# A linear-attention and MLP block: duplicated 64-row tails in one DMA, and a new order of the first loads and key projections

## The chip, the cores and the metric

The kernel runs on one core of a Trainium2 chip. The metric is the device time of one execution in microseconds. Each kernel is timed in several runs, and the median is given. A separate, profiled execution supplies the trace.

## The reference

Two blocks work on the same x (2048 tokens, 576 features) and are mixed by a gate. All numbers are float32.

```python
def _A_ref(x, wqkv, wo):                       # 32 heads of 18
    qkv = (x @ wqkv).reshape(B, S, 3, H, Dh).transpose(2, 0, 3, 1, 4)
    q, k, v = qkv[0], qkv[1], qkv[2]
    phi = lambda t: jnp.where(t > 0, t + 1, jnp.exp(t)) + 1e-6
    pq, pk = phi(q), phi(k)
    kv = jnp.einsum("bhsd,bhse->bhde", pk, v)
    z = jnp.einsum("bhsd->bhd", pk)
    o = jnp.einsum("bhqd,bhde->bhqe", pq, kv) / (jnp.einsum("bhqd,bhd->bhq", pq, z)[..., None] + 1e-6)
    return o.transpose(0, 2, 1, 3).reshape(B, S, D) @ wo
def _B_ref(x, w1, b1, w2, b2):                 # 576 -> 4608 -> 576
    h = _gelu(_layernorm(x) @ w1 + b1)
    return h @ w2 + b2
g = _sigmoid((x * gate_w).sum(-1, keepdims=True))
return g * _A_ref(...) + (1 - g) * _B_ref(...)
```

## The kernel before, in words

**Stages.** The kernel first projects x to keys and queries, 16 tiles of 128 tokens one after the other, and sums keys against x on the way; from those sums it makes the attention matrix. The MLP follows, in a scheme with seven products in place of eight; it takes most of the time, and its order of instructions comes from a planner in the program. The change lies in the first 30 us or so and in the loads of the x tiles.

**Precision.** Each operand of a product is split into a high part, rounded by ScalarE (ACT), and a low part, the remainder, made by VectorE (DVE); three products (high by high, low by high, high by low) are summed in PSUM. `split_x` and `split_w` do that for a tile of x and for a half of a weight.

**Rows.** The 576 features are five blocks along the partitions: four of 128 rows, and a tail of 64. The tail is held twice, in partitions 0 to 63 and 64 to 127, so that one matmul serves two of the three products. `load_twice` (line 146) loads it: two DMAs from the same 64 rows of HBM, one into each half of the partitions. It is used by `load_x` (the tail `xe` of a tile), by `load_w` (the tail `we` of a half of the key or query weights, 288 columns) and by `load_wv`. The main part of a tile comes from `xm`, that of a weight half from `wm`. In the profile the tile of x is called `t`, the raw weights are `s`, and their split forms both lie in `y`. A related helper, `four_times` (line 150), describes 32 rows that are read four times, by an access pattern whose first dimension is 4 with stride 0; it serves `load_pair`, whose tails (`accs<-in_xe`) are loaded in a later stage, and the tails of the MLP weights.

**Order.** Every engine runs its instructions in program order: the class `InOrder` (line 110) records each one, so that nearly all have line 120 in the profile, and tiles tell them apart. DMAs are issued from SyncE's queue (SP), from ACT's, and a few from GpSimd's (POOL). Issues by SP and ACT together take eight completion semaphores in turn, so that the ninth waits for the landing of the first.

**The start.** Line 457 and those after it issue the first loads: the first x tile on SP, the first half of the key weights in pieces on ACT, the table load of ACT, then on SP two more x tiles, the second key half, the two query halves, and two tiles of x by rows (`xn`). A set of products of one tile by one half of a weight is 14 matmuls (`project`; `first_keys` names the tile, the half and the PSUM bank). `first_keys` of three tiles by the first half come first, then the column of the gate is put beside the second key half, that half is split, and its keys follow. For the second key half the operand is 290 columns wide, for the others 288, which tells them apart in the profile. `both_phi` takes the keys of a tile through phi, by ACT and DVE.

Of the kernel before, what the change touches and what calls it, by code (L numbers as in the profile page):

```python
# [93 lines left out]
def raw(ap):  # L94
    return ap.bitcast(F32)
# [31 lines left out]
def tile_gated_mix(ctx: ExitStack, tc: tile.TileContext, x, xm, xe, wm, we, wvm, wve, wo, um, ue, w2, b1, b2, gw, out):  # L127
    nc = tc.nc
    pe, act, dve, pool = (InOrder(tc, e) for e in (nc.tensor, nc.scalar, nc.vector, nc.gpsimd))
# [14 lines left out]
        return ps[:, next(ff_banks)]  # L144

    def load_twice(dst, src, by=sp):
        for half in range(2):
            by.dma_start(dst[half * 64:(half + 1) * 64], src)

    def four_times(ap, half):  # L150

# [45 lines left out]
    QUERY, KEY = range(2)  # L197
    TERMS = ((0, 0), (0, 1), (1, 0))
    W, at_ = {}, 0
    for part in (KEY, QUERY):  # L200
        for half in range(2):
            n = HALF + 2 * (part == KEY and half)
# [20 lines left out]
    def load_w(part, half, pieces=((0, 5),), by=sp):  # L223
        if (part, half) not in wraw:
            wraw[part, half] = wsp.tile([P, 5, HALF + 2], F32, name="s", tag="s")
        s = wraw[part, half]
        main = wm[part * 2 + half].rearrange("p (t n) -> p t n", t=4)
        tail = we[part * 2 + half]
        for t0, t1 in pieces:
            if t0 < 4:  # L230
                by.dma_start(s[:, t0:min(t1, 4), :HALF], main[:, t0:min(t1, 4)])
            if t1 == 5:
                load_twice(s[:, 4, :HALF], tail, by)

    def split_w(part, half, by=dve, pieces=((0, 5),)):
        w = W[part, half]
        s = wraw[part, half][:, :, :w.shape[2]]
        for t0, t1 in pieces:
            act.activation(w[:, t0:t1], s[:, t0:t1], AF.Copy)
            by.tensor_tensor(out=w[:, 5 + t0:5 + t1], in0=s[:, t0:t1], in1=raw(w[:, t0:t1]), op=OP.subtract)  # L240

    def load_x(i):
        xraw[i] = yt.tile([P, 5, P], F32, name="t")
        sp.dma_start(xraw[i][:, 0:4], xm[i].rearrange("p (t n) -> p t n", t=4))
        load_twice(xraw[i][:, 4], xe[i])

    def split_x(i, pieces=((0, 5),), on_dve=False):
        if i not in xs:
            xs[i] = x_places[PLACE[i] % X_RING]
        to, src = xs[i], xraw[i]  # L250
        for t0, t1 in pieces:
            if on_dve:
                dve.tensor_copy(to[:, t0:t1], src[:, t0:t1])
            else:
                act.activation(to[:, t0:t1], src[:, t0:t1], AF.Copy)
            if t0 < 4:
                dve.tensor_sub(to[:, 5:9], src[:, 0:4], raw(to[:, 0:4]))
            if t1 == 5:
                dve.scalar_tensor_tensor(to[:, 4], raw(to[:, 4]), low_half[:, 0:1], src[:, 4], op0=OP.mult, op1=OP.add)
# [12 lines left out]
    def project(i, part, half, order=BY_ROWS, n=None, between={}):  # L272
        w = W[part, half]
        p = banks[i, part, half] = ps[:, next(halves_in) if n is None else n]
        for m, (a, b) in enumerate(order):
            pe.matmul(p[:, :w.shape[2]], xs[i][:, a, :], w[:, b], start=(m == 0), stop=(m == len(order) - 1))
            if m in between:
                between[m]()
# [16 lines left out]
    def keys_phi(i, half):  # L295
        if half == 0:
            K[i] = kp.tile([P, D], F32, name="k")
        phi(K[i], i, KEY, half, (lambda: None, lambda: sums_of_x(i))[half])
# [156 lines left out]
    first = ORDER[:FIRST]  # L455
    gwr = spare[0:1, :5 * P]
    load_x(first[0])
    load_w(KEY, 0, ((0, 1), (1, 2), (2, 4)), act)
    pool.dma_start(gwr[:, :D], gw.rearrange("(a n) -> a n", a=1))
    pool.dma_start(gwr[:, D:], gw[4 * P:D].rearrange("(a n) -> a n", a=1))  # L460
    act.activation(tiny, ones[:, 0:1], AF.Exp)
    load_w(KEY, 0, ((4, 5),), act)
    load_x(first[1])
    load_x(first[2])
    load_w(KEY, 1)
    load_w(QUERY, 0)
    load_xn(first[0])
    load_w(QUERY, 1)
# [12 lines left out]
    def first_keys(n, half, between={}):  # L481
        project(first[n], KEY, half, HI_FIRST, 3 * half + n, between)
# [4 lines left out]
    def both_phi(n):  # L487
        for half in range(2):
            keys_phi(first[n], half)
# [13 lines left out]
    first_keys(0, 0, {0: lambda: warm(1), 1: lambda: warm(1), 2: lambda: warm(1), 3: turn_gate})  # L503
    split_x(first[1])
    first_keys(1, 0)
    split_x(first[2])
    first_keys(2, 0)
    dve.tensor_copy(wraw[KEY, 1][:, :, HALF:HALF + 1], column[:, :, None])
    dve.memset(wraw[KEY, 1][:, :, HALF + 1:HALF + 2], 1.0)
    split_w(KEY, 1)  # L510
    load_x(ORDER[3])
    first_keys(0, 1)
    first_keys(1, 1)
    split_w(QUERY, 0)
    both_phi(0)
    first_keys(2, 1)
    both_phi(1)
    keys_split(first[0])
# [54 lines left out]
    def load_wv():  # L573
        sp.dma_start(wv[:, 0:4], wvm.rearrange("p (t n) -> p t n", t=4))
        load_twice(wv[:, 4], wve)
# [1082 lines left out]
```

## Time and profile before

| | |
|---|---|
| median of 3 runs | 1093.72 us (1092.69 to 1094.6) |
| profiled execution | 1095.47 us |
| its span, first to last instruction | 1093.8 us |
| granted TensorE clock, mean | 0.998 |
| PE busy | 1084.9 us (99%) |
| DVE, ACT, POOL busy | 933.3, 692.3, 219.4 us |
| DMA | 189.72 MB, mean 173 GB/s |

PE is TensorE's matmuls, PEld its weight loads, SPq and ACTq are queues that issue DMAs. A row of the timeline gives the start and the length in us, then the engine, line, operation, out<-in by the program's names and how many were merged; in square brackets stands the engine's idle time just before, and what ended it. A row of a table of windows gives, after the window and its length, the busy time of PE, PEld, DVE, ACT and POOL with their instructions in brackets, the granted TensorE clock, the mean busy share of 16 DMA engines, and GB/s.

### The profile page before, as it was taken

The numbers are of one execution on the slowest core, as the hardware profiler recorded it, in microseconds if no ns is written. First come the engines' busy times: TensorE is split into PE (matmuls) and PEld (weight loads), VectorE is DVE, ScalarE is ACT, GpSimd is POOL, SyncE is SP. The second block draws the span as 40 slices with busy tenths as digits, with TensorE's granted clock in tenths as the row PEclk, the third lists the DMA queues.
The fourth block names the chain that finished last, engine by engine and source line by source line (L and its number), as shares of the span: only waits on it lengthen the run. The fifth ranks groups of instructions, "written<-read, shape, count | busy, mean of one in ns | idle before, by whom it ended". The sixth has DMA issues, their size and how long they took to land.

```text
span 1093.8 us, 18578 instructions
## 1 busy us (share of the span) xinstructions
PE 1084.9 (99%) x6712; PEld 998.0 (91%) x6712; DVE 933.3 (85%) x1583; ACT 692.3 (63%) x1228; POOL 219.4 (20%) x212
## 2 busy tenths in 40 slices
PE   8999999999999999999999999999999999999998
PEld 7999999999898989998999989999899998999898
DVE  5568787797699999899999898988887887989888
ACT  5677767444568787787887785555645555455542
POOL 1111112431222321233120221021221221111110
PEclk9999999999999999999999999999999999999999
DMA  6457673654755565744565559664544445444432
GB/s 178 123 98 192 169 176 141 237 217 166 230 181 188 193 218 192 254 174 158 214 216 207 188 192 396 199 233 118 151 132 118 130 123 146 132 121 119 142 90 88
DMA packets 109006, 189.72 MB, mean 173 GB/s; under 512 B 8940, under 2 KB 68604, under 8 KB 104818
## 3 DMA queue, kind: packets, MB, share of 16 engines
q1 hardware_dynamic: 108002, 187.78, 53.6%
q8 instruction: 53, 0.87, 0.4%
q10 hardware_dynamic: 720, 0.74, 0.2%
q14 instruction: 39, 0.32, 0.1%
q0 software_dynamic: 192, 0.01, 0.0%
HBM read 121.70 MB, written 66.80 MB: 172 GB/s over the span
## 4 chain that ended last, share of the span: by engine, by line
PE 96%; ACT 1%; DMA 1%; DVE 1%; issue 0%; SPq 0%; ACTq 0%; DVEq 0%
PE ps L120 96%; DMA s<-in_we 1%; DMA s<-in_wm 0%; ACT e L120 0%; ACT L120 0%; ACT y L120 0%; SPq L120 0%; DVE ks L120 0%; DVE y L120 0%; ACT ks L120 0%; ACTq L120 0%; ACT ys L120 0%; DVE xs L120 0%; DVE wp L120 0%; ACT xn L120 0%
## 5 line engine op out<-in xcount | busy, mean ns | idle before, releaser
L120 PEld LDWEIGHTS ps<-region,h 128*128 128x128 f32 x3072 | 436.5, 188 | 24.5 <-ACT ps L120 0.4
L120 PE MATMUL ps<-region,h 128*128 128x288 f32 x3072 | 452.3, 295 | 0.0
L120 DVE TENSOR_TENSOR accs<-ps,accs 128x576 f32<-128x576 f32 x334 | 245.3, 752 | 25.1 <-PE ps L120 19.4
L120 PE MATMUL ps<-y,wa 128*128 128x512 f32 x1008 | 255.4, 392 | 0.0
L120 PEld LDWEIGHTS ps<-y,wa 128*128 128x128 f32 x1008 | 181.8, 188 | 31.8
L120 PE MATMUL ps<-y,wb 128*128 128x512 f32 x756 | 199.4, 393 | 0.0
L120 DVE TENSOR_TENSOR h<-u,h 128x512 fp32r<-128x512 f32 x240 | 166.0, 711 | 31.5 <-ACT u L120 28.7
L120 POOL TENSOR_TENSOR fresh<-fresh 128x288 f32<-128x288 f32 (+1 forms) x98 | 85.7, 876 | 394.3 <-DVE h L120 167.7
L120 PEld LDWEIGHTS ps<-y,wb 128*128 128x128 f32 x756 | 133.8, 188 | 20.7
L120 PE MATMUL ps<-y 128*128 128x288 f32 (+2 forms) x950 | 135.6, 299 | 4.1 <-ACT y L120 3.3
L120 PEld LDWEIGHTS ps<-y 128*128 128x128 f32 (+1 forms) x950 | 131.2, 190 | 7.0 <-ACT y L120 3.9
L120 ACT ACTIVATE region<-fresh 128x576 fp32r<-128x576 f32 (+1 forms) x132 | 80.3, 625 | 69.3 <-PE ps L120 65.2
L120 POOL TENSOR_TENSOR u<-u 128x512 f32<-128x512 f32 x54 | 72.2, 1337 | 221.7 <-DVE h L120 140.0
L120 ACT ACTIVATE ps<-ps 128x576 f32<-128x576 f32 (+1 forms) x125 | 77.5, 623 | 50.8 <-PE ps L120 36.2
L120 DVE TENSOR_TENSOR region<-fresh,region 128x576 fp32r<-128x576 f32 (+1 forms) x132 | 88.9, 692 | 2.1 <-ACT region L120 2.0
L120 ACT ACTIVATE u<-ps 128x512 f32<-128x512 f32 x73 | 43.4, 594 | 69.4 <-PE ps L120 67.4
L120 ACT ACTIVATE h<-u 128x512 fp32r<-128x512 f32 x128 | 75.0, 620 | 9.4 <-POOL u L120 4.8
L120 ACT ACTIVATE h<-u,b1s 128x512 fp32r<-128x512 f32 x73 | 52.6, 722 | 35.6 <-DVE u L120 35.5
L120 PE MATMUL ps<-wp,qt 128*128 128x288 f32 x448 | 63.0, 297 | 0.0
L120 PEld LDWEIGHTS ps<-wp,qt 128*128 128x128 f32 x448 | 59.8, 188 | 0.0
L120 DVE TENSOR_TENSOR u<-ps,u 128x512 f32<-128x512 f32 x74 | 50.5, 683 | 6.3 <-ACT u L120 5.1
L120 DVE TENSOR_TENSOR u<-u 128x512 f32<-128x512 f32 x74 | 51.4, 695 | 2.5 <-POOL u L120 1.6
(140 smaller groups left out, 1054.3 us busy)
## 6 DMA issues: line engine op xcount, KB each, us to landing
w1d<-wa SPq DMA_DIRECT2D x17, 1280.0 KB
wa<-w1d SPq DMA_DIRECT2D x68, 320.0 KB
fresh<-in_w SPq DMA_DIRECT2D x70, 288.0 KB
y<-yd SPq DMA_DIRECT2D x14, 1280.0 KB
w1d<-wb SPq DMA_DIRECT2D x17, 960.0 KB
wb<-w1d SPq DMA_DIRECT2D x51, 320.0 KB
yd<-ystage SPq DMA_DIRECT2D x28, 320.0 KB
fresh<-in_um SPq DMA_DIRECT2D x64, 128.0 KB
```

What stands on the lines that cost most here:

```text
L120: self.last = self.tc.keep_in_program_order(op(*args, **kwargs))
```

## The change

`load_twice` issues one DMA in place of two: its source pattern gets a first dimension of 2 with stride 0 ahead of the 64 rows. This holds for all 16 x tiles, for the four halves of key and query weights and for the value weights. Pieces 2 to 4 of the first key half go to SP's queue, and the tail of that half moves ahead of ACT's table load. The second key half is issued ahead of the third x tile. The third tile's split and its keys by the first half move behind the second key half's split, and `both_phi` of the first tile ahead of the split of the first query half.

```diff
     def load_twice(dst, src, by=sp):
-        for half in range(2):
-            by.dma_start(dst[half * 64:(half + 1) * 64], src)
+        (ld, r), (st, n) = src.ap
+        by.dma_start(dst, bass.AP(tensor=src.tensor, offset=src.offset, ap=[[0, 2], [ld, r], [st, n]]))
...
     load_x(first[0])
-    load_w(KEY, 0, ((0, 1), (1, 2), (2, 4)), act)
+    load_w(KEY, 0, ((0, 1), (1, 2)), act)
+    load_w(KEY, 0, ((2, 4),))
+    load_w(KEY, 0, ((4, 5),), act)
     pool.dma_start(gwr[:, :D], gw.rearrange("(a n) -> a n", a=1))
     pool.dma_start(gwr[:, D:], gw[4 * P:D].rearrange("(a n) -> a n", a=1))
     act.activation(tiny, ones[:, 0:1], AF.Exp)
-    load_w(KEY, 0, ((4, 5),), act)
     load_x(first[1])
+    load_w(KEY, 1)
     load_x(first[2])
-    load_w(KEY, 1)
     load_w(QUERY, 0)
...
     split_x(first[1])
     first_keys(1, 0)
-    split_x(first[2])
-    first_keys(2, 0)
     dve.tensor_copy(wraw[KEY, 1][:, :, HALF:HALF + 1], column[:, :, None])
     dve.memset(wraw[KEY, 1][:, :, HALF + 1:HALF + 2], 1.0)
     split_w(KEY, 1)
+    split_x(first[2])
     load_x(ORDER[3])
     first_keys(0, 1)
     first_keys(1, 1)
+    both_phi(0)
     split_w(QUERY, 0)
-    both_phi(0)
+    first_keys(2, 0)
     first_keys(2, 1)
```

On SP's queue the start of the program stood like this before; t_168, t_181 and t_185 are the first three x tiles, s_189 is the second key half, s_193 and s_199 are the query halves:

```order
L120 DMA t_168<-in_xm 128x512
L120 DMA t_168<-in_xe 64x128 x2
L120 DMA t_181<-in_xm 128x512
L120 DMA t_181<-in_xe 64x128 x2
L120 DMA t_185<-in_xm 128x512
L120 DMA t_185<-in_xe 64x128 x2
L120 DMA s_189<-in_wm 128x4x288
L120 DMA s_189<-in_we 64x288 x2
L120 DMA s_193<-in_wm 128x4x288
L120 DMA s_193<-in_we 64x288 x2
```

It now stands like this; t_168, t_179 and t_185 are the x tiles, s_171 is the first key half, s_182 the second, s_188 the first query half:

```order
L120 DMA t_168<-in_xm 128x512
L120 DMA t_168<-in_xe 128x1x128
L120 DMA s_171<-in_wm 128x2x288
L120 DMA t_179<-in_xm 128x512
L120 DMA t_179<-in_xe 128x1x128
L120 DMA s_182<-in_wm 128x4x288
L120 DMA s_182<-in_we 128x1x288
L120 DMA t_185<-in_xm 128x512
L120 DMA t_185<-in_xe 128x1x128
L120 DMA s_188<-in_wm 128x4x288
L120 DMA s_188<-in_we 128x1x288
```

Each pair of 64-row transfers has become one of 128 rows, a part of the first key half has come in as the third issue, and the second key half has moved from the tenth and later issues to the sixth and seventh, ahead of the third x.

On PE the projections at the start of the program (288 columns: first key half, or query; 290 columns: second key half) were and are, with the rows of before marked - and those of the change +:

```order
-L120 MATMUL ps<-y 128x288 x38
-L120 MATMUL ps<-y 128x290 x42
+L120 MATMUL ps<-y 128x288 x24
+L120 MATMUL ps<-y 128x290 x28
+L120 MATMUL ps<-y 128x288 x14
+L120 MATMUL ps<-y 128x290 x14
 L120 MATMUL ps<-y 128x288 x42
```

The 14 matmuls of the third tile by the first key half have moved behind 28 of the second key half.

## Prediction

> **What bounds the kernel now.** I read the busy shares first, then the chain that ended last in order of time, then the timelines of TensorE (PE) and of SyncE's queue (SPq) over the first 30 us, then the DMA issues of the first 20 us with their sizes, and last a table of windows with the DMA share. The busy line of the page:
>
> ```profile
> PE 1084.9 (99%) x6712; PEld 998.0 (91%) x6712; DVE 933.3 (85%) x1583; ACT 692.3 (63%) x1228; POOL 219.4 (20%) x212
> ```
>
> PE is the bound. It leaves about 9 us of the span of 1093.8 us idle, so little can be won, and only where PE waits; whatever makes PE later there is paid in full. The chain in order of time (start, length, what) shows where that is:
>
> ```profile
> 9.16 5.51 DMA s<-in_we
> ...
> 14.74 1.42 ACT y L120
> ...
> 16.19 1.68 DVE y L120
> ...
> 17.91 4.35 PE ps L120 x19
> ...
> 28.11 62.01 PE ps L120 x409
> ```
>
> A DMA, the last 64-row tail of the second key half (s<-in_we), is issued at 9.16 and lands at 14.67; ACT and DVE split that weight half in two, PE goes on, and from 28.11 the chain is PE alone. Everything that the change moves lies ahead of that. PE's own timeline:
>
> ```profile
> 8.52 5.32 PE L120 MATMUL ps<-y 128*128 128x288 f32 x38
> 16.21 1.49 PE L120 MATMUL ps<-y 128*128 128x290 f32 x9 [2.37 <-ACT y L120]
> 17.91 9.95 PE L120 MATMUL ps<-y 128*128 128x290 f32 x61 [0.22 <-DVE y L120]
> 28.11 2.13 PE L120 MATMUL ps<-y 128*128 128x288 f32 x14 [0.25 <-DVE accs L120]
> ```
>
> The 38 matmuls end the keys of three tiles with the first key half (14 each), at 5.32/38 = 0.14 us apiece. Then PE stands 2.37 us for the second half, and the 70 matmuls behind it (three tiles by that half, two by the first query half) end at 27.86. So the landing at 14.67 sets the end. Why it is late, SP's queue shows (64-row transfers go out in twos, "x2"):
>
> ```profile
> 4.84 0.74 SPq L120 DMA_DIRECT2D t<-in_xm  x1
> 6.70 1.11 SPq L120 DMA_DIRECT2D t<-in_xe  x2
> 7.85 0.60 SPq L120 DMA_DIRECT2D s<-in_wm  x1
> 8.49 1.27 SPq L120 DMA_DIRECT2D s<-in_we  x2
> ```
>
> The third x stands ahead of the second key half, each issue takes about 0.6 us, and from 5.58 to 6.70 the queue waits. The DMA engines run dry for it (window, length, engines, clock, DMA share, GB/s):
>
> ```profile
> 3.00:4.00 1.00, 1.00 (x6) 1.00 (x6) 0.00 (x0) 0.71 (x2) 0.86 (x4) 1.00 1.00 349
> 6.00:7.00 1.00, 0.84 (x6) 0.65 (x6) 0.99 (x3) 0.75 (x3) 0.00 (x0) 1.00 0.93 176
> 8.00:9.50 1.50, 1.50 (x14) 1.36 (x13) 1.05 (x3) 1.18 (x3) 0.00 (x0) 1.00 0.36 62
> 17.92:21.34 3.42, 3.42 (x14) 3.42 (x15) 2.44 (x3) 3.01 (x9) 0.25 (x1) 0.50 0.62 179
> ```
>
> Full load is 349 GB/s; at 8.0 to 9.5 only 62 GB/s move. The last row is kept for later: after its pause PE runs 3.42 us at clock 0.50.
>
> **The change part by part.** *One transfer for both halves.* It halves the issues of the tails, some 0.55 to 0.6 us of SP time for each, and that looks like the gain. But its source now begins with a dimension of 2 with stride 0. The trace has a relative of it: the loads of accs<-in_xe in a later stage read 32 rows four times with a leading 4. They are issued at 68.31 and 70.26, and this is the DMA load when they are what is left to move:
>
> ```profile
> 68.31 1.28 SPq L120 DMA_DIRECT2D accs<-in_xe  x2
> 70.26 2.32 SPq L120 DMA_DIRECT2D accs<-in_xe  x2
> 73.20:74.20 1.00, 1.00 (x10) 1.00 (x9) 1.00 (x3) 0.77 (x2) 0.00 (x0) 1.00 0.30 79
> ```
>
> A share of 0.30 of 16 engines is four to five of them, and 79 GB/s is less than half of the 176 GB/s and 0.93 at 6 to 7 us, when plain 64-row tails of the same row length are among what moves. I read from this that a leading dimension of 4 puts the transfer on four engines, and that a leading 2, which no row of before has, will put it on two. The Trainium skill goes that step too, in "DMA: Bandwidth & Descriptors", section "Why a DMA increments its semaphore by 16 and not by 1": the hardware's descriptor generator takes the largest number of engines up to 16 that divides the slowest dimension of both access patterns. By that rule the new form gets two engines; the trace's four-fold form agrees with 0.30, and a leading 2 it does not show.
>
> The sizes, by the DMA issues of the first 20 us (KB for each issue, and for one of them the us to its landing):
>
> ```profile
> s<-in_wm SPq DMA_DIRECT2D x3, 576.0 KB
> t<-in_xm SPq DMA_DIRECT2D x4, 256.0 KB
> s<-in_we SPq DMA_DIRECT2D x6, 72.0 KB
> s<-in_wm ACTq DMA_DIRECT2D x2, 144.0 KB
> s<-in_wm ACTq DMA_DIRECT2D x1, 288.0 KB
> t<-in_xe SPq DMA_DIRECT2D x8, 32.0 KB
> accs<-in_gw POOLq DMA_DIRECT2D x1, 2.2 KB, 4.0
> ```
>
> Until the second key half has landed, the changed queue moves main parts of two x and two weight halves, 2*256 + 2*576 = 1664 KB over 16 engines, 104 KB each, and the tails 2*64 + 2*144 = 416 KB over two engines, 208 KB each. The two loaded engines so carry 312 KB, 319.5 thousand bytes; before, with the third x, it is 150 KB on each of 16. One engine moves 349/16 = 21.8 GB/s at full load, 79/4 = 19.8 GB/s by the four-engine row: 14.7 to 16.2 us. SP's issues, seven of 0.6 us, are out by about 5.5 us, so these two engines never run dry. The first packets move at about 2.0 us by this row:
>
> ```profile
> 0.00:2.00 2.00, 0.87 (x4) 0.87 (x5) 0.34 (x5) 0.00 (x0) 1.09 (x11) 1.00 0.05 14
> ```
>
> The second key half then lands at 16.7 to 18.2 us instead of 14.67; I take 17.2, nearer the full-load rate, since wide rows make most of it: **+2.5 us** (+2.0 to +3.5). ACT's 1.42 and DVE's 1.68 behind it stay.
>
> *First weights on two queues.* Pieces 2 to 4 go from ACT's to SP's queue, the tail ahead of ACT's table load. That spares ACT its last issues ahead of the first split, but the first x's tail and this tail now lie on the two engines: 16 + 32 + 36 + 72 = 156 KB, 7.3 us, landed at about 9.3, and the second x 48 KB later, at 11.6. PE's run of 38, which starts at 8.52 now, starts some 2 us later, and the keys of two tiles end by about 15 (16.5 at half clock), ahead of PE's restart at 17.2 + 1.5 = 18.7 (14.67 to 16.21 is 1.5 now). This costs **0**, covered by that wait; without it, it would be the 2 us.
>
> *Second key half ahead of the third x, and the third tile's keys behind it.* Before, 14 matmuls of the third tile by the first half lie ahead of PE's 2.37 us gap; now they lie behind the restart, where PE has no gap: 14*0.14 = **+2.0 us**. In the queue the third x comes 16 + 32 = 48 KB, 2.3 us, after the second key half; its split stands on ACT right behind that half's split and on DVE likewise, and the key phi of the first tile queues behind it. PE reaches the third tile only after 28 matmuls, some 5.8 us after its restart (at the half clock that the window showed): covered.
>
> *What is late next.* The first query half follows with 16 + 32 + 36 + 72 = 156 KB, 7.3 us, after the second key half; its splits, the first two rows below, end 1.41 + 1.66 us later, 10.4 us after that landing. PE is there after 1.5 + 7.7 + 2.0 = 11.2 us (7.7 is 27.86 - 28*0.14 - 16.21): covered by 0.8 us, at the low rate by nothing, but the first nine matmuls of a tile need only the high part, 1.66 us earlier. On ACT the phi of the second and third tile stand behind that split; their banks are not written again before the third tile's queries. Then come an xn of 18 KB and the second query half, 126 KB or 5.9 us more, landed at 30.4; its split (third row) moves from 30.84 to 35.
>
> ```profile
> 17.14 1.41 ACT L120 ACTIVATE y<-s 128x1440 fp32r<-128x1440 f32 x1 [0.98 <-DMA s<-in_we]
> 18.58 1.66 DVE L120 TENSOR_TENSOR y<-s,y 128x1440 fp32r<-128x1440 f32 x1 [0.72 <-ACT y L120]
> 30.84 1.39 ACT L120 ACTIVATE y<-s 128x1440 fp32r<-128x1440 f32 x1
> 16.99 1.11 SPq L120 DMA_DIRECT2D t<-in_xe  x2
> 38.54 0.72 ACT L120 ACTIVATE y<-t 128x640 fp32r<-128x640 f32 x1
> ```
>
> The fourth x (last two rows) is split 20 us after its issue. The two engines' backlog behind the second key half, 140 KB of mains and 208 KB of tails up to that x, is 16.3 us: landed at 33.5, covered. The two short PE waits, 0.22 us here and 0.25 us at 28.11, for ACT and DVE work that has now more time, may go: **-0.2** (0 to -0.5). The half clock came after a pause of 2.37 us; the pause is now 4 us or so, and I leave the 1.7 us that it cost unchanged (bounds: another 1.7, or 1.7 saved).
>
> Sum: 2.5 + 0 + 2.0 - 0.2 = **+4.3 us**. The profiled execution took 1095.47 us with a span of 1093.8, 1.67 us around it; it would take 1099.8. The median of the runs is 1.75 us below it, 1093.72, so I forecast 1098.0. Bounds of the terms: 2.0 + 2.0 - 0.5 - 1.7 = +1.8, and 3.5 + 2.0 + 1.7 = +7.2.
>
> **The rivals.** *All 16 engines still move a tail (faster).* Then the second key half is issued by about 5.4 us and 2080 KB at 349 GB/s take 6.1 us from 2.0 on; allowing from issue to landing the 4.0 us of the small transfer in the sizes above, it lands at about 9.5. PE's gap goes, the half clock with it: 11.2 restart, 84 matmuls of 0.14, end at 23.0 instead of 27.86, less what phi holds back: -4.5 us, 1089.2. For it speaks that SP's issues and the dry stretch at 8 us are really the cause of the landing at 14.67; against it the row with 0.30. The Trainium skill's "Rules for kernel authors" of the same page speaks for the change: two transfers to disjoint partition halves should be one over 128 partitions. The point that decides is the number of engines: the landing has to come by 13.0 to pay for the 2.0 us less waits, 11.0 us at 21.8 GB/s or 234 KB, and 104 + 416/k falls under it from k = 4 on.
>
> *Two engines, but hidden (no change).* The lower bounds together, above all a restart of PE at full clock: +1.8, 1095.5. The landing alone cannot hide it, since 14 matmuls are behind the gap in any case.
>
> *More than the head (slower still).* PE's longer pauses double the half-clock stretch (+1.7), and the two engines, which also carry the four-fold tails of the later stage, make a pair of tiles or the fourth x late by 2 us: about +8, 1101.7. Against it: the pairs' loads stand ahead of the x tails in the queue, not behind.
>
> **How the numbers follow.** Forecast 0.71, all engines 0.11, hidden 0.10, worse 0.08. About 0.2% (2.2 us) is what a measurement of this kernel can tell from no change, so faster is 0.11, same 0.10, slower 0.79. The range runs from 1095.2 to 1101.3: it takes in the forecast's bounds and most of the hidden case, and leaves out the fast one and most of the worst.
>
> **What would show it.** In the changed profile: SP's issues up to the second key half done before 7 us; windows between 9 and 17 us with a DMA share near 0.13 and about 40 GB/s; the split of the 128x1450 weights on ACT at 16.7 to 18.5; a PE gap of 3 us or more ahead of the first 128x290 matmul; the 14 matmuls of 128x288 between those of 128x290; the last of the first query half's second tile near 32. It is wrong if the tails move at a share of 0.9, or if ACT's split starts before 13 us.

## The result, and the profile after

The changed kernel takes 1099.08 us (median of 6 runs, 1098.41 to 1099.99) against 1093.95 us before (6 runs, 1092.45 to 1094.6): a ratio of 1.005 with a 95% interval of 1.0037 to 1.0063. It is slower by 5.1 us. The forecast was 1098.0 us in a range of 1095.2 to 1101.3. The profiled execution took 1099.48 us with a span of 1097.8 us, 4.0 us more than the profiled one of before on both counts.

The chain that ended last, in order of time (start, length, what), leads through the same load as before, with other numbers:

```profile
5.92 11.67 DMA s<-in_we
...
17.70 1.42 ACT y L120
...
19.16 70.95 PE ps L120 x467
```

The tail of the second key half is issued at 5.92, 3.2 us earlier than before, and yet lands at 17.59 instead of 14.67. From 19.16 on the chain is PE alone. PE's timeline:

```profile
11.31 6.12 PE L120 MATMUL ps<-y 128*128 128x288 f32 x24
19.16 15.05 PE L120 MATMUL ps<-y 128*128 128x290 f32 x98 [1.73 <-ACT y L120]
```

PE restarts at 19.16 instead of 16.21, 2.95 us later. The 98 matmuls behind that (the third tile's 14 by the first key half among them, and the third tile's queries) end at 34.21; before, the 84 that stood there ended at 28.11 + 2.13 = 30.24. From restart to that point it is 15.05 us now and 14.03 us then, 1.02 us more. 2.95 and 1.02 are 3.97 us, the whole difference of the two spans. Nothing behind 34 us adds to it.

How the tails move shows in windows of the first part (window, length, busy time of PE, PEld, DVE, ACT, POOL, then clock, DMA share, GB/s):

```profile
10.00:11.00 1.00, 1.00 (x7) 0.75 (x6) 0.40 (x1) 0.00 (x0) 0.00 (x0) 0.50 0.14 45
14.00:15.00 1.00, 1.00 (x6) 1.00 (x5) 0.86 (x4) 0.00 (x0) 0.00 (x0) 0.50 0.14 48
28.00:29.00 1.00, 1.00 (x9) 1.00 (x8) 1.00 (x3) 0.97 (x3) 0.25 (x1) 1.00 0.14 47
9.90:16.73 6.83, 6.83 (x29) 6.17 (x29) 2.00 (x6) 1.18 (x2) 0.00 (x0) 0.50 0.34 96
20.14:23.56 3.42, 3.42 (x15) 3.13 (x14) 1.99 (x5) 2.30 (x7) 0.00 (x0) 0.50 0.74 249
```

Wherever a tail is what is left, the share of 16 engines is 0.14, a little over two of them, and 45 to 48 GB/s move. Full load is 349 GB/s in the row shown of before. That is the load of two engines. The last two rows are the stretches at half clock: PE ran 6.83 us of the first keys at clock 0.50, where nothing waited for it, and 3.42 us behind its restart, as long as in the profile of before.

### The profile page after: what moved, and what is told of

It is laid out like the page before. It is cut to its first block, busy times and chain, and to the rows that moved or that the text cites. A ratio compares the mean times of both kernels' runs of the same rounds, so it can differ in the third digit from the quotient of the medians.

```text
span 1097.8 us, 18543 instructions
## 1 busy us (share of the span) xinstructions
PE 1088.2 (99%) x6712; PEld 1002.3 (91%) x6712; DVE 931.0 (85%) x1583; ACT 692.2 (63%) x1228; POOL 219.9 (20%) x212
## 4 chain that ended last, share of the span: by engine, by line
PE 98%; DMA 1%; ACT 0%; SPq 0%; DVE 0%; issue 0%; ACTq 0%
PE ps L120 98%; DMA s<-in_we 1%; DMA s<-in_wm 0%; SPq L120 0%; ACT y L120 0%; DVE wp L120 0%; ACT wp L120 0%; DVE ystage L120 0%; ACTq L120 0%
## 5 line engine op out<-in xcount | busy, mean ns | idle before, releaser
L120 PE MATMUL ps<-y 128*128 128x288 f32 (+2 forms) x950 | 138.2, 303 | 4.3 <-ACT y L120 4.1
L120 PEld LDWEIGHTS ps<-y 128*128 128x128 f32 (+1 forms) x950 | 133.7, 194 | 6.9 <-ACT y L120 4.7
```

Source lines behind the costliest of these rows:

```text
L120: self.last = self.tc.keep_in_program_order(op(*args, **kwargs))
```

## The experiments

The theory is that of the prediction: the leading 2 puts each tail on two DMA engines, the bytes queued on these two set the landing of the second key half, and the third tile's matmuls behind PE's restart are paid in full. The rival is that the new order costs and the one transfer is harmless. "Before" in the ratios is the kernel before, run on the same chip: a median of 1093.29 to 1093.50 us in the three series of 15 to 27 runs.

**The two parts apart.** In the first run, two_dmas, the old body of `load_twice` stands in the changed kernel; in the second, one_dma_alone, the new body stands in the kernel before, by the reverse of this diff.

```diff
     def load_twice(dst, src, by=sp):
-        (ld, r), (st, n) = src.ap
-        by.dma_start(dst, bass.AP(tensor=src.tensor, offset=src.offset, ap=[[0, 2], [ld, r], [st, n]]))
+        for half in range(2):
+            by.dma_start(dst[half * 64:(half + 1) * 64], src)
```

> The changed kernel with its tails loaded by two 64-row DMAs again, all of the new order kept. Theory (the one-transfer form sits on two DMA engines): the load share between 9 and 17 us goes back up, the second key half's split starts on ACT at 11 to 13 us instead of 17.70, PE restarts at 12.5 to 14.5 and, with the third tile's 14 matmuls behind, the time is 1090 to 1092.5, faster than before. Rival (the new order is what costs, the one transfer is harmless): the time stays at 1098 to 1100.

Measured: 1092.71 us, ratio 0.9999 (0.9991 to 1.0008). ACT's split of the second key half and PE's restart:

```profile
12.60 1.41 ACT L120 ACTIVATE y<-s 128x1450 fp32r<-128x1450 f32 x1 [3.44 <-DMA s<-in_we]
```
```profile
14.06 1.51 PE L120 MATMUL ps<-y 128*128 128x290 f32 x9 [1.93 <-ACT y L120]
```
```profile
10.00:11.00 1.00, 1.00 (x10) 1.00 (x9) 0.24 (x3) 0.00 (x0) 0.00 (x0) 1.00 0.94 294
```

With two DMAs again, the window from 10 to 11 us has a share of 0.94 in place of 0.14, the split starts 5.1 us earlier and the whole loss is gone. The order alone, with the first weights on two queues, does not cost anything. It does not gain anything either that could be told from no change; the theory had 1090 to 1092.5.

> The kernel before with only the one-transfer form of the tails, the old order kept. Theory (two engines): they carry 120 KB of mains and 240 KB of tails until the second key half has landed, 17 to 18.5 us from 2.0 on; its split starts at 19 to 20.5, PE restarts about 4.5 us late with no matmuls moved behind, and the time is 1097 to 1099.5. Rival (the order costs): 1092 to 1094, as before or a little better for the issues that are saved.

Measured: 1102.9 us, ratio 1.0088 (1.0074 to 1.0101), 3.4 us over the top of what the theory said. The split of the second key half and that of the first query half on ACT, and PE's wait later:

```profile
19.60 1.42 ACT L120 ACTIVATE y<-s 128x1450 fp32r<-128x1450 f32 x1 [3.20 <-DMA s<-in_we]
24.25 1.41 ACT L120 ACTIVATE y<-s 128x1440 fp32r<-128x1440 f32 x1 [3.24 <-DMA s<-in_we]
```
```profile
34.34 2.05 PE L120 MATMUL ps<-y 128*128 128x288 f32 x7 [2.64 <-DVE accs L120]
```

The start of the split is where the theory put it (19 to 20.5). What it missed is the next thing that is late: in the old order the split of the first query half stands on ACT ahead of the first tile's phi, ACT stands 3.24 us for that half's tail, and the phi behind it makes PE wait 2.64 us. So the one transfer alone costs 9.6 us, and the new order takes back 3.8 us of that. The rival has it the wrong way round.

**The phi alone.** To see whether that wait is ACT's order, one line is moved in one_dma_alone.

```diff
+    both_phi(0)
     split_w(QUERY, 0)
-    both_phi(0)
```

> The kernel before with the one-transfer tails (old order) and one part of the new order: the phi of the first tile's keys ahead of the split of the first query half. In the run without it ACT stands 3.24 us for that half's tail with the phi queued behind it, PE stops 2.64 us at 34.34 for a bank that phi empties, and runs at half clock behind that. Theory (ACT's program order makes the late query half PE's wait): that wait goes below 0.5 us and the half clock with it, 1098 to 1100. Rival (phi is late by itself, since the loads are): 1102 to 1103.5, as without it.

Measured: 1099.24 us, ratio 1.0048 (1.0034 to 1.0062). The same place on PE:

```profile
32.04 2.13 PE L120 MATMUL ps<-y 128*128 128x288 f32 x14 [0.16 <-DVE accs L120]
```

The wait of 2.64 us is down to 0.16, and with it 3.7 us are gone, about what the whole new order gave back. With two-engine tails, moving phi ahead is worth as much as the whole new order; the rest of it comes out even.

**One transfer on all engines.** The source is read row by row, each row twice, so that its slowest dimension is 64 and not 2. The two copies of a row then lie in neighbouring partitions, so the mask of `split_x` and the tail of the gate's row get that order too, and the value weights keep their two DMAs (`load_halves`, the old body of `load_twice`). rows_first is the changed kernel with this, rows_first_old_order the kernel before.

```diff
-        by.dma_start(dst, bass.AP(tensor=src.tensor, offset=src.offset, ap=[[0, 2], [ld, r], [st, n]]))
+        by.dma_start(dst, bass.AP(tensor=src.tensor, offset=src.offset, ap=[[ld, 64], [0, 2], [st, n]]))
...
+    odd = spare[:, 6 * P:6 * P + 64]
+    pool.memset(odd, -1.0)
+    pool.affine_select(odd, odd, pattern=[[-2, 64]], compare_op=OP.is_ge, fill=0.0, base=-1, channel_multiplier=1)
+    pool.affine_select(odd, odd, pattern=[[2, 64]], compare_op=OP.is_ge, fill=0.0, base=1, channel_multiplier=-1)
+    dve.tensor_reduce(out=low_tail, in_=odd, op=OP.add, axis=AX.X)
...
+    gwt = spare[0:1, 8 * P:9 * P]
+    pool.tensor_copy(gwt.rearrange("p (a t r) -> p a t r", a=64, t=2),
+                     gwr[:, 4 * P:D].rearrange("p (a r) -> p a r", r=1)[:, :, None, :].to_broadcast([1, 64, 2, 1]))
...
-        load_twice(wv[:, 4], wve)
+        load_halves(wv[:, 4], wve)
```

> The changed kernel with one transfer for both copies still, but with the source read row by row, each row twice (64 rows first, then the copy), so that the slowest dimension is 64 and the copies lie in neighbouring partitions; a mask and a reordered gate row go with it, made by GpSimd at the start. The value weights' tail is loaded by two DMAs. Theory (the leading 2 is the cause): all 16 engines, the second key half is split from 9.5 to 11 us on, 1088.5 to 1091. Rival (one transfer that reads each row twice is slow whatever its leading dimension): 1097 to 1100.

Measured: 1091.02 us, ratio 0.9975 (0.9967 to 0.9984).

```profile
10.36 1.42 ACT L120 ACTIVATE y<-s 128x1450 fp32r<-128x1450 f32 x1 [1.22 <-DMA s<-in_we]
```
```profile
9.24 16.57 PE L120 MATMUL ps<-y 128*128 128x288 f32 x122
```
```profile
10.00:11.00 1.00, 1.00 (x10) 1.00 (x9) 0.22 (x3) 0.64 (x1) 0.00 (x0) 1.00 1.08 343
```

With the same bytes in the same number of transfers up to here, but another leading dimension, the window moves 343 GB/s instead of 45. PE has no pause for the second key half any more: 122 matmuls run from 9.24 on in one piece at full clock. This is the fast case of the prediction in kind, though not in size: it is 2.3 us faster than before, where 4.5 us were said, and just above the 1088.5 to 1091 us of the theory. It is 8.1 us faster than the changed kernel.

> The kernel before, its old order, with the row-by-row form of the one transfer. Theory: issues are saved and 16 engines move the tails, the second key half is split at 11 to 12.5 us and the third tile's 14 matmuls stay ahead of it: 1089.5 to 1092, within 1.5 us of the same form in the new order. Rival (the order costs by itself): faster than the same form in the new order by 2 us or more.

Measured: 1092.06 us, ratio 0.9988 (0.9979 to 0.9997). PE's long run of keys and queries there, and the piece behind it:

```profile
10.16 14.54 PE L120 MATMUL ps<-y 128*128 128x288 f32 x104 [0.24 <-ACT y L120]
24.94 2.13 PE L120 MATMUL ps<-y 128*128 128x288 f32 x14 [0.23 <-DVE accs L120]
```

That is just above the theory's 1089.5 to 1092 us. On 16 engines the new order is the better one by 1.0 us, which is the opposite of what the rival needs; which part of it brings that, the first weights below show.

**The dose.** The theory says that bytes on two engines count, so the tails are given the one transfer in turn: those of x alone (x_tails_one, the first line of the diff in the changed kernel), and those of the weights alone (w_tails_one, the second).

```diff
-                load_twice(s[:, 4, :HALF], tail, by)
+                load_halves(s[:, 4, :HALF], tail, by)
...
-        load_twice(xraw[i][:, 4], xe[i])
+        load_halves(xraw[i][:, 4], xe[i])
```

> The changed kernel, its order kept; the x tails keep the one transfer with the leading 2, the tails of all weights are loaded by two 64-row DMAs again. Theory (the bytes on the two engines set the landing): until the second key half has landed these carry 104 KB of mains, 64 KB of x tails and 18 KB of weight tails, 186 KB; at the 20.5 GB/s that the changed kernel shows (319.5 thousand bytes in 15.6 us) that is 9.3 us, and with the issues that come back the split starts at 12 to 13 us: 1092 to 1094. Rival (each one-transfer tail costs the same, by its form and not by its bytes): half of the way between the kernels, 1095.5 to 1097.

> The reverse of the run before: weight tails by the one transfer with the leading 2, x tails by two 64-row DMAs. Theory: 104 + 144 + 8 = 256 KB on the two engines, 12.8 us at 20.5 GB/s, the split of the second key half at 14.5 to 15.5 us: 1095 to 1097.5. Rival (equal cost of each transfer): the same time as its reverse, within 0.5 us.

Measured: 1093.42 us, ratio 0.9998 (0.9989 to 1.0007), for x alone, and 1095.38 us, ratio 1.0022 (1.0013 to 1.0031), for the weights alone. The split of the second key half in the first:

```profile
13.05 1.42 ACT L120 ACTIVATE y<-s 128x1450 fp32r<-128x1450 f32 x1 [1.51 <-DMA s<-in_we]
```

and in the second:

```profile
15.53 1.42 ACT L120 ACTIVATE y<-s 128x1450 fp32r<-128x1450 f32 x1 [3.28 <-DMA s<-in_we]
```

Two transfers of either kind lie ahead of the landing, so equal cost by form would have made the two runs equal. They differ by 2.0 us in the sense of their bytes, and both times lie where the theory put them. Set beside each other, with KB on the two loaded engines until the second key half has landed, worked out as in the prediction:

| tails by the leading 2 | KB on each of the two | split starts, us | time, us |
|---|---|---|---|
| none (two_dmas) | 130 | 12.60 | 1092.71 |
| x | 186 | 13.05 | 1093.42 |
| weights | 256 | 15.53 | 1095.38 |
| both (the change) | 312 | 17.70 | 1099.08 |
| both, third x ahead (one_dma_alone) | 360 | 19.60 | 1102.9 |

From 186 KB on each further KB costs: 174 KB, 178 thousand bytes, in 6.55 us, 27 GB/s for an engine. That is more than the 22.5 to 24 GB/s for each of two engines in the windows where tails alone are left (45 to 48 GB/s), so the count of KB puts the runs in order but is not exact; what it leaves out stays open. With few KB the issues matter: the row-by-row form has the same 130 KB as the two DMAs and splits 2.2 us earlier, and its tail of the second key half is issued by 5.71, that of two_dmas by 8.03.

**The first weights.** Priced at nothing, under the wait for the second key half. They go back to one queue in the changed kernel (first_weights_back) and in rows_first (rows_weights_back).

```diff
-    load_w(KEY, 0, ((0, 1), (1, 2)), act)
-    load_w(KEY, 0, ((2, 4),))
-    load_w(KEY, 0, ((4, 5),), act)
+    load_w(KEY, 0, ((0, 1), (1, 2), (2, 4)), act)
...
     act.activation(tiny, ones[:, 0:1], AF.Exp)
+    load_w(KEY, 0, ((4, 5),), act)
```

> The changed kernel with the first weights back on one queue: pieces 2 to 4 on ACT's queue and the tail of the first key half behind ACT's table load. Theory (covered by the wait for the second key half, since the two engines carry the same bytes either way): 1098.4 to 1099.8, no difference that can be told. Rival (the two queues bring the start forward, or push the second key half back): off by 1.5 us or more, either way.

Measured: 1099.45 us, ratio 1.0058 (1.0046 to 1.0071), 0.4 us over the changed kernel, which the scatter of the runs does not tell from nothing. The cover shows on PE, which here stops 6.46 us inside the first keys and yet ends the queries of the third tile at 35.04, 0.83 us later than the changed kernel; the two profiled executions are as far apart (1100.29 and 1099.48 us):

```profile
16.36 18.68 PE L120 MATMUL ps<-y 128*128 128x288 f32 x118 [6.46 <-ACT y L120]
```

> The fastest form so far (new order, rows read twice one by one on 16 engines) with the first weights back on one queue, the tail of the first key half behind ACT's table load. There PE has no wait for the second key half that would cover the first weights. Theory (their two queues pay once that cover is gone): 0.3 to 1.2 us slower than that form, 1091.3 to 1092.2. Rival (it is still nothing): 1090.8 to 1091.2.

Measured: 1093.09 us, ratio 0.9994 (0.9985 to 1.0002), 2.1 us slower than the row-by-row form. The direction is as expected, the size is nearly twice the top of what was said. The tail of the first key half is split at 10.24 here:

```profile
10.24 0.44 ACT L120 ACTIVATE y<-s 128x288 fp32r<-128x288 f32 x1 [2.04 <-DMA s<-in_we]
```

In rows_first the pieces 2 to 4 and that tail are split in one go, over at 8.44:

```profile
7.42 1.02 ACT L120 ACTIVATE y<-s 128x576 fp32r<-128x576 f32 x2 [2.21 <-DMA s<-in_wm]
```

So this part of the change is worth 2.1 us where all engines move the tails, and in the changed kernel nearly all of that lies under the wait for the two engines. It also says what the new order is worth on 16 engines: rows_weights_back has all of it but the first weights, and its 1093.09 us are 1.0 us more than the 1092.06 us of the old order. By these medians, from two series, the first weights are the gain, and the rest of the new order costs about 1 us.

**The third tile's matmuls.** A second set of 14 is put where the change put the first, in the changed kernel.

```diff
     first_keys(2, 0)
+    first_keys(2, 0)
```

> The changed kernel with the third tile's 14 matmuls by the first key half done twice, behind the second key half. Theory (PE has no slack behind its restart, so a set of 14 that stands there is paid in full): 14 times 0.14 us, 1.8 to 2.2 us on top of the changed kernel, 1100.9 to 1101.4. Rival (PE waits there for phi or for the first query half in any case, and a set of matmuls is hidden): 1098.6 to 1099.8.

Measured: 1100.83 us, ratio 1.0069 (1.0056 to 1.0082), 1.75 us over the changed kernel, a hair below what was expected, and outside the rival's range.

```profile
20.72 14.01 PE L120 MATMUL ps<-y 128*128 128x290 f32 x103 [0.22 <-DVE y L120]
```

PE runs through: 103 matmuls in one piece from 20.72. A set that stands behind the restart is paid. The profile alone would say less, a span of 1098.5 us against 1097.8: in this execution those 103 ran at full clock, at 0.14 us apiece, where the profile of the changed kernel has its 3.42 us at half clock.

**A second profile of before.** The two profiles differ by 4.0 us and the medians by 5.1.

> The kernel before, unchanged, for a second profile. Its first profiled execution took 1095.47 us, 1.5 us over the median of its runs, with PE at clock 0.50 for 3.42 us behind its gap and a granted clock of 0.998. Theory (that stretch and a late landing in that one execution are why the two profiles differ by 4.0 us and the medians by 5.1): at a granted clock of 1.000 no half-clock stretch ahead of 30 us and 1092 to 1093.5 us; at 0.998 the stretch is there and 1094.5 to 1095.7. Rival (the difference is only scatter of the runs): the time does not follow the clock.

Measured: 1091.91 us in one execution, at a granted clock of 1.000 and with a span of 1090.2 us. The split of the second key half, PE's timeline, and the window that had the clock at 0.50 in the first profile of before:

```profile
12.03 1.42 ACT L120 ACTIVATE y<-s 128x1450 fp32r<-128x1450 f32 x1 [1.59 <-DMA s<-in_we]
```
```profile
8.44 6.56 PE L120 MATMUL ps<-y 128*128 128x288 f32 x47
15.21 8.46 PE L120 MATMUL ps<-y 128*128 128x290 f32 x61 [0.21 <-DVE y L120]
25.00 2.13 PE L120 MATMUL ps<-y 128*128 128x288 f32 x14 [1.32 <-DVE accs L120]
```
```profile
17.92:21.34 3.42, 3.42 (x27) 3.42 (x27) 2.19 (x6) 2.90 (x10) 1.18 (x2) 1.00 0.22 67
```

The half starts its split 2.7 us earlier than in the first profile, and PE does 27 matmuls in the window where it did 14. More than that, the pause of 2.37 us, from which the prediction started, is not there: 47 matmuls run in one piece, the first nine of the second key half among them, and the set that ended at 30.24 in the first profile ends at 27.13. Against this execution the profile of the changed kernel, with 34.21, is 7.1 us late and not 4.0. The granted clocks of the 27 runs of before in the first series bear it out in part: four have 0.998, and these took 1095.16 to 1095.66 us; five with 0.999 took 1092.88 to 1094.48, and the 18 with 1.000 took 1091.96 to 1094.28, a spread that the clock does not account for. The first profile of before, 1095.47 us at 0.998, was one of the late ones. The six runs of the changed kernel all lie between 0.995 and 0.998.

## Why the prediction was right, point by point

- **Two engines.** Right, and it decided the sign. A leading 4 that took a share of 0.30 in a later stage was the only sign in the profile of before. With the leading 2 the share is 0.14 where tails are left, and with a leading 64 it is 1.08 in a window in which such tails and main parts move. What the Trainium skill states in "DMA: Bandwidth & Descriptors", section "Why a DMA increments its semaphore by 16 and not by 1", agrees with these shares for 2, 4 and 64. The advice of the Trainium skill in the same page's "Rules for kernel authors", to make one 128-partition transfer of two to disjoint partition halves, stood behind the fast rival. In this kernel it paid with a leading 64 and not with a leading 2: in the old order the one is 1.2 us faster than before (rows_first_old_order), the other 9.6 us slower (one_dma_alone).
- **The landing.** 17.2 us was said, within 16.7 to 18.2; it is 17.59, by 319.5 thousand bytes in 15.6 us, 20.5 GB/s. The term is +2.9 us and not +2.5, against the landing at 14.67 of one late execution. Against before_again, where the split starts at 12.03, the split of the changed kernel is 5.7 us later. The reading that this landing sets the end of the kernel before is true of the first profile; in the second PE comes to that half without a pause.
- **The third tile.** +2.0 us was said, less 0.2 for waits that go. keys_twice gives 1.75 us for such a set. Between the two profiles only 1.02 us come out net; the two waits that were there before, 0.22 and 0.25 us, are no longer on the chain, which leaves about 0.3 us that no row accounts for.
- **First weights, at nothing.** Right, for the reason that was given (first_weights_back). Without the cover it was said to cost 2 us. No run shows that for two-engine tails; with the row-by-row form, where the cover is gone, it is a gain of 2.1 us (rows_weights_back).
- **What is late next.** The first query half was to land at 24.5, 7.3 us behind the second key half, and to be covered by the matmuls that PE had left. It is split from 24.76 on, right behind its landing, and PE does not wait:

```profile
24.76 1.41 ACT L120 ACTIVATE y<-s 128x1440 fp32r<-128x1440 f32 x1 [1.28 <-DMA s<-in_we]
```

- **Phi ahead of that split, without a term.** The prediction gave no price to this part of the change. In the old order it is worth 3.7 us: one_dma_alone shows the same lateness without it, 2.64 us of PE and, with the clock, 3.7 us in the time, and phi_first is rid of both. That nothing had to be added here may rest on it; no run takes it out of the changed kernel.
- **The half clock.** Left at 0 by the first profile of before, in which it had struck. Between the two profiles that is right, 3.42 us in each. Against the median it is not: most runs of before have none, and all of the changed kernel's have some. Together with the late landing in that same profile this can make the 1.1 us by which the medians differ more than the profiles; the two were not separated. The step that was short is the subtraction of 1.75 us to get from the profiled execution to the median, as if that scatter were the same in both kernels. So the close match of the sum, 4.3 us said and 4.0 us measured, is one between two particular executions, and the median is 1.1 us above the forecast.
- **Two signs that were off.** SP's issues up to the second key half were to be out by 7 us, and PE's pause ahead of it to be 3 us or more. The issues end at 8.38 (below), and the pause is 1.73 us, since the first keys ran at half clock till 16.73 and ended at 17.4, not 15 to 16.5. They also began late: PE's run of 24 starts at 11.31, where some 2 us behind 8.52 was said, and the tail of the first key half is split at 11.98, where a landing at 9.3 was said. The cover over that part was thinner than it was said to be.
- **The rivals.** The fast one could be had, by another leading dimension, at about half the gain that was said. That 4 engines would be enough to break even was not tried. The worse one, with x pairs late further on, did not come: nothing behind 34 us adds.

## What to carry to other kernels

Fewer DMAs are no gain if the access pattern of the one that is left begins with a small dimension, as with the 2 here: look for the DMA share of a transfer of that form anywhere in the profile, and put the dimension with many entries first. Cost such a transfer by the bytes queued on its few engines, with everything else that these must carry, and not by its own size. And before a sum is made against one profiled execution, compare its time and granted clock with those of the other runs.

## What the runs showed of the hardware that was not expected

In the changed kernel, where two engines have a backlog, the issues of DMAs themselves become long. SP's take up to 3.43 us, those of main parts, which all engines move, among them:

```profile
4.22 1.66 SPq L120 DMA_DIRECT2D s<-in_wm  x1
5.92 2.46 SPq L120 DMA_DIRECT2D s<-in_we  x1
8.42 3.43 SPq L120 DMA_DIRECT2D t<-in_xm  x1
11.90 0.52 SPq L120 DMA_DIRECT2D t<-in_xe  x1
```

The same transfers in the row-by-row form, with no such backlog:

```profile
4.23 0.57 SPq L120 DMA_DIRECT2D s<-in_wm  x1
4.85 0.86 SPq L120 DMA_DIRECT2D s<-in_we  x1
5.76 0.67 SPq L120 DMA_DIRECT2D t<-in_xm  x1
6.47 0.54 SPq L120 DMA_DIRECT2D t<-in_xe  x1
```

Part of that may be waiting for a semaphore that the profile counts to the issue; the runs do not tell it apart for certain. Against it speaks that in the profile of before such a wait stands as a gap between two issues (5.58 to 6.70), while these follow each other within 0.04 to 0.05 us. Either way the queue behind a slow transfer stands still as well, so the transfers for all 16 engines are issued late too: that of the third x is out at 11.85 here and at 6.43 there.
